# Decode attention with its softmax in two parts and K moved in 8 MB loads

## The chip, the cores and the metric

The kernel runs on 1 core of a Trainium2 chip. The metric is the device time of one execution in microseconds (us). Times of two kernels are compared on the same chip, round by round. PE is the engine for matrix products, DVE is VectorE, ACT is ScalarE, POOL is GpSimd; SyncE issues the loads, and 16 DMA engines move them. PSUM is the memory that PE writes to. PV is the product of the softmax's exponentials with V. A load has landed when the parts of all 16 DMA engines are there.

## The reference, cut to what matters

A decode step of one transformer block, batch 2, one new token, model width 1024, 32 query heads over 4 K/V heads, and a cache of 32768 tokens, all in bf16:

```python
mod = (silu(c) @ w_mod)                       # 12.6 MB of weights
h   = layernorm(x) * (1 + ca) + sa
q   = h @ wq                                  # 8.4 MB
scores = einsum('bhqd,bhkd->bhqk', q, k) * Dh ** -0.5
p   = softmax(scores, axis=-1)
o   = einsum('bhqk,bhkd->bhqd', p, v)         # K and V: 67 MB each
x   = x + ga * (o @ wo)                       # 8.4 MB
...                                           # MLP: w1 and w2, 7.3 MB each
```

The 2 x 4 pairs of batch and K/V head are called groups here, numbered 0 to 7. A group has 8 MB of K and 8 MB of V, and serves 8 query heads. Nothing is read twice, so 178 MB must come from HBM.

## The kernel before

All large loads are issued in one order by SyncE into one arena of 160 KB per partition. K has two buffers of 32 KB, one per half; V has one of 64 KB. A load is issued when the last reader of its place has finished (`frees`):

```python
def add_k(i, hf):   # two loads of 4 MB
    add(("K", i, hf), [2, TPC * D], ...[hf], hf * 32 * KB, f"K{hf}")
def add_v(i):       # one load of 8 MB
    add(("V", i), [NCH, TPC * D], ..., 64 * KB, "V")
for i in range(NBG):
    add_k(i, 0); add_k(i, 1); add_v(i)
# ... wo, w1, w2 follow in the same stream
T.dma("sp", ..., key=cur.sem, writes=[cur.reg], frees=old)
```

In a group, 32 steps transpose 8 blocks of K on PE, copy them out of PSUM (20 on DVE, 12 on ScalarE) and multiply them by q. After each quarter (8 steps) the scores are copied and their maximum is taken. When all four quarters are there, the softmax follows, then PV:

```python
for cc in range(NCH):
    for g8 in range(TPC // 8):
        tr(i, cc, g8)                  # transposes and evacuation
        ...
        qk(*pipe.pop(0))               # three steps later
softmax_1(); softmax_2(); softmax_3()  # one maximum over all 32768 tokens
for cc in range(NCH): exp(cc)
for cc in range(NCH):
    part_sum(cc)
    pv(i, cc)                          # 16 matmuls a quarter
row_sums(); extract(); extract_2(i)
```

## Time and profile before

| | before |
|---|---|
| time, median of 4 runs (range) | 420.06 us (419.99 to 420.11) |
| span of the profiled run | 418.7 us |
| load packets, as a share of 16 DMA engines' span | 98.8% |
| V landings, groups 2 to 7, distance | 38.63 to 38.71 us |
| last weight load landed; end of the kernel | 415.76; 418.69 us |

One row of the page: what the DMA engines moved in each fortieth of the span.

```profile
GB/s 373 450 380 449 448 404 493 398 406 446 441 432 429 423 451 429 419 454 457 391 435 476 407 416 448 438 438 426 438 438 426 416 460 457 377 448 428 424 427 249
```

It stays around 430 (373 to 493) until the last slice. That one holds the 3 us of compute after the last load.

### The profile page before, as it was taken

How to read it: one execution, taken by the hardware profiler on the slowest of the kernel's cores; microseconds unless marked ns; L12 is line 12 of the kernel's file. 1: busy time of each engine (PE TensorE's matmuls, PEld its weight loads, DVE VectorE, ACT ScalarE, POOL GpSimd, SP SyncE). 2: the span in 40 equal slices, each digit the busy share in tenths (PEclk: the TensorE clock that was granted, in tenths of full speed). 3: DMA queues.
4: the chain of work that ended last, by engine and by line, in shares of the span. 5: the costliest groups of instructions: out<-in, count | busy, mean ns of one | idle time of the engine just before them, and what ended most of it. 6: DMA issues, size and time to landing. Idle time of an engine off the chain costs nothing.

```text
span 418.7 us, 11609 instructions
## 1 busy us (share of the span) xinstructions
PE 291.0 (70%) x5183; PEld 231.3 (55%) x5183; DVE 209.6 (50%) x423; ACT 149.4 (36%) x179; POOL 6.8 (2%) x29
## 2 busy tenths in 40 slices
PE   1407449766996895699369957976995699564536
PEld 1104219762993794299149926962894399221214
DVE  1201105546677676467726664766477567620411
ACT  2000015533565364256405632643365166400100
POOL 3000000000000000000000000000000000000000
PEclk9999557986896997799589958986697889576585
DMA  9989999999999999999999999999999999899995
GB/s 373 450 380 449 448 404 493 398 406 446 441 432 429 423 451 429 419 454 457 391 435 476 407 416 448 438 438 426 438 438 426 416 460 457 377 448 428 424 427 249
DMA packets 5581, 178.42 MB, mean 426 GB/s; under 512 B 698, under 2 KB 706, under 8 KB 964
## 3 DMA queue, kind: packets, MB, share of 16 engines
q1 hardware_dynamic: 5572, 178.28, 98.8%
q8 instruction: 8, 0.13, 0.1%
q14 instruction: 1, 0.01, 0.0%
HBM read 178.28 MB, written 0.00 MB: 426 GB/s over the span
## 4 chain that ended last, share of the span: by engine, by line
DMA 71%; PE 24%; DVE 2%; issue 1%; ACT 1%; SPq 1%
DMA V<-in_A_v_cache_dram 39%; DMA wo<-in_A_wo_dram 10%; DMA K<-in_A_k_cache_dram 10%; PE psZ L584 10%; DMA w<-in_B_w_dram 9%; PE psKT L536 8%; DMA wmod<-in_w_mod_dram 4%; PE psS L548 1%; PE psZ L548 1%; PE psS L655 1%; PE psZ L729 1%; PE psZ L469 1%; ACT KT_sb L540 0%; PE psS L469 0%; DVE m1c L553 0%
## 5 line engine op out<-in xcount | busy, mean ns | idle before, releaser
L536 PE MATMUL psKT<-ident,K 128*128 128x128 bf16 x2048 | 163.1, 229 | 11.5 <-DMA K<-in_A_k_cache_dram 11.5
L540 ACT ACTIVATE KT_sb<-psKT 128x1024 bf16<-128x1024 bf16 x96 | 98.2, 1025 | 124.4 <-PE psKT L536 124.4
L542 DVE COPY KT_sb<-psKT 128x1024 bf16<-128x1024 bf16 x160 | 106.7, 688 | 61.6 <-PE psKT L536 61.2
L536 PEld LDWEIGHTS psKT<-ident,K 128*128 128x128 bf16 x2048 | 126.7, 102 | 13.0 <-DMA K<-in_A_k_cache_dram 12.7
L584 PE MATMUL psZ<-V,E_sb 128*32 128x512 bf16 x512 | 46.4, 541 | 23.2 <-DMA V<-in_A_v_cache_dram 20.0
L548 PE MATMUL psS<-qcur,KT_sb 128*128 128x8 bf16 x1024 | 44.7, 167 | 2.2 <-issue 2.2
L584 PEld LDWEIGHTS psZ<-V,E_sb 128*32 128x32 bf16 x512 | 18.7, 130 | 47.7 <-issue 38.8
L548 PE MATMUL psZ<-qcur,KT_sb 128*128 128x8 bf16 x1024 | 43.0, 167 | 2.2 <-issue 1.5
L548 PEld LDWEIGHTS psS<-qcur,KT_sb 128*128 128x128 bf16 x1024 | 40.0, 97 | 2.3 <-issue 2.3
L548 PEld LDWEIGHTS psZ<-qcur,KT_sb 128*128 128x128 bf16 x1024 | 37.9, 96 | 3.4 <-issue 1.6
L572 ACT ACTIVATE E_sb<-S_sb 128x512 bf16<-128x512 f32 x32 | 19.5, 630 | 29.6 <-DVE S_sb L570 29.6
L570 DVE TENSOR_TENSOR S_sb<-S_sb,gmb 128x512 f32<-128x512 f32 x32 | 20.0, 685 | 0.3
L576 DVE TENSOR_REDUCE rs<-E_sb 128x8 f32<-128x512 bf16 x32 | 19.7, 675 | 0.0
L469 PE MATMUL psS<-wmod,inT 128*32 128x512 bf16 x32 | 5.1, 624 | 16.2 <-DMA wmod<-in_w_mod_dram 16.2
L553 DVE TENSOR_REDUCE m1c<-psZ 128x8 f32<-128x512 f32 x16 | 11.1, 693 | 10.2 <-ACT S_sb L552 10.1
L595 DVE RECIPROCAL rinv<-psM 128x1 f32<-128x1 f32 x8 | 1.3, 168 | 27.7 <-PE psM L593 27.7
L605 PE MATMUL psM<-msum,hmat 128*128 128x128 f32 x16 | 4.2, 347 | 13.3 <-DVE msum L600 13.3
L559 PE MATMUL psM<-identf,m 128*8 128x128 f32 x16 | 4.3, 369 | 13.1 <-DVE m L556 13.1
L553 DVE TENSOR_REDUCE m1c<-psS 128x8 f32<-128x512 f32 x16 | 11.1, 693 | 3.2 <-ACT S_sb L552 3.1
L552 ACT ACTIVATE S_sb<-psZ 128x512 f32<-128x512 f32 x16 | 9.5, 595 | 7.5 <-PE psZ L548 7.5
L477 DVE COPY S_sb<-psS 128x512 f32<-128x512 f32 x1 | 0.7, 690 | 22.9 <-PE psS L469 22.9
L469 PEld LDWEIGHTS psS<-wmod,inT 128*32 128x32 bf16 x32 | 1.1, 132 | 19.3 <-DMA wmod<-in_w_mod_dram 18.0
(123 smaller groups left out, 167.5 us busy)
## 6 DMA issues: line engine op xcount, KB each, us to landing
K<-in_A_k_cache_dram SPq DMA_DIRECT2D x16, 4096.0 KB, 27.1
wq<-in_A_wq_dram SPq DMA_DIRECT2D x2, 4096.0 KB, 44.8
wo<-in_A_wo_dram SPq DMA_DIRECT2D x2, 4096.0 KB, 39.0
w<-in_B_w_dram SPq DMA_DIRECT2D x2, 3584.0 KB, 32.5
wmod<-in_w_mod_dram SPq DMA_DIRECT2D x1, 6144.0 KB, 29.8
w<-in_B_w_dram SPq DMA_DIRECT2D x3, 2048.0 KB, 37.8
wmod<-in_w_mod_dram SPq DMA_DIRECT2D x1, 4608.0 KB, 15.8
wmod<-in_w_mod_dram SPq DMA_DIRECT2D x1, 1536.0 KB, 6.0
```

The source lines that it names most:

```text
L469: pe(lambda e, w=it.view, k=k, kk=kk, ch=ch, n=n, q=q: e.matmul(bank[n][32 * q:32 * q + 32, :], lhsT=inT[:, k, :], rhs=w[:, kk, ch * 512:( ...
L536: pe(lambda e, kq=kq, jj=jj, w=kt, t=t: e.transpose(psKT[kq][:, jj * 128:(jj + 1) * 128], w[:, t, :], ident[:, :]), reads=[it.reg, "ident" ...
L540: act(lambda e, src=src: e.activation(KT_sb[g8][:, :, :], src, ACT.Copy), reads=[f"psKT{kq}"], writes=[f"KT_sb{g8}"], sem=f"ev{cc}_{g8}")
L542: dve(lambda e, src=src: e.tensor_copy(KT_sb[g8][:, :, :], src), reads=[f"psKT{kq}"], writes=[f"KT_sb{g8}"], sem=f"ev{cc}_{g8}")
L548: pe(lambda e, t=t, jj=jj: e.matmul(ps[:, t * HPG:(t + 1) * HPG], lhsT=KT_sb[g8][:, jj, :], rhs=qcur[:, :], start=True, stop=True), reads= ...
L552: act(lambda e: e.activation(Sc, ps.rearrange("p (t h) -> p h t", h=HPG), ACT.Copy), reads=[preg], writes=[f"S_sb_{cc}"], sem=f"sc{cc}")
L553: dve(lambda e: e.tensor_reduce(m1c[:, :, cc], ps.rearrange("p (t h) -> p h t", h=HPG), AX.X, ALU.max), reads=[preg], writes=[f"m1c{cc}"])
L559: pe(lambda e: e.matmul(psM[0:HPG, 0:128], lhsT=m1[:, :], rhs=identf[:, :], start=True, stop=True), reads=["m1", "identf"], writes=["psM"])
L570: dve(lambda e: e.tensor_tensor(Sc, Sc, gmb[:, :].unsqueeze(2).to_broadcast([128, HPG, TPC]), ALU.subtract), reads=[f"S_sb_{cc}", "gmb"], ...
L572: act(lambda e: e.activation(Ec, Sc.rearrange("p h (u t) -> p u h t", t=4), ACT.Exp, scale=SCALE), reads=[f"S_sb_{cc}"], writes=[f"E_sb_{c ...
L576: dve(lambda e: e.tensor_reduce(rs4[:, :, cc], Ec.rearrange("p u h t -> p h u t"), AX.XY, ALU.add), reads=[f"E_sb_{cc}"], writes=[f"rs4_{c ...
L584: pe(lambda e, t4=t4, tg=tg, q=q: e.matmul(psO[32 * q:32 * q + 32, :], lhsT=E_sb[:, tg // 4, :, :].rearrange("p h t -> p (h t)"), rhs=vt[: ...
```

## The change

Its intent is to move K in 8 MB loads, like V, and to make up for what that costs in time for the compute. A whole K in one buffer has to be free as a whole: so DVE copies the second half aside (four copies of 4096 elements per partition), and the transposes of the last two quarters read the copy. Compute then starts only when all 8 MB are there. So that V's buffer is free in time all the same, the first three quarters get their own maximum, and their PV runs beside the softmax of the last quarter. Both PV sums are joined with weights exp(m_part - m).

```diff
-    def add_k(i, hf):
-        add(("K", i, hf), [2, TPC * D], ...[hf], hf * 32 * KB, f"K{hf}")
+KEEP = {(0, 1): 0, (0, 5): 1, (1, 3): 2, (2, 1): 3}      # step after which each copy stands
+    def add_k(i):
+        if i:
+            add(("K", i), [NCH, TPC * D], rows, 0, "K", view=kv)      # 8 MB
+        else:                                                         # group 0: two halves
+            add(("K", i), ... rows[:, 0:2, :], 0, sem="K", ...)
+            add(("K2", i), ... rows[:, 2:4, :], 32 * KB, sem="K2", ...)
...
+    def keep(i, n):
+        dve(lambda e: e.tensor_copy(kc[:, n // 2, lo:lo + 32 * D], kv[:, 2 + n // 2, lo:lo + 32 * D]), ...)
...
-            act(... S_sb copy of the quarter ...)
-            dve(... maximum of the quarter ...)
+            dve(... maximum of the quarter ...)
+            act(... S_sb copy of the quarter ...)
...
-        softmax_1(); softmax_2(); softmax_3()
-        for cc in range(NCH): exp(cc)
-        for cc in range(NCH):
-            part_sum(cc); pv(i, cc)
-        row_sums(); extract(); extract_2(i)
+        exp(0); exp(1)                  # the maximum of quarters 0 to 2 was taken during quarter 3
+        ...                             # rest of the scores
+        exp(2); pv(i, 0); max_2(1); pv(i, 1); max_3(1); exp(3); weights(); pv(i, 2)
+        ...                             # part sums, weights_2
+        row_sums(); extract(0); pv(i, 3); row_sums_2(); extract(1); extract_2(i)
```

Evacuations are now 16 on DVE and 16 on ScalarE per group, and some weight loads at the end have other places in the arena.

More of the change, by code (lines that the diff above doesn't have):

```diff
@@ L34 @@
 RING = 160 * 1024
+KC_AT = 128 * 1024
 AHEAD = ("sc2", "sc3", "pk", "ac")
 WMOD_ITEMS = ((0, 1), (1, 4), (4, 8))
-W2_ITEMS = ((0, 8, 96), (8, 16, 112), (16, 24, 128), (24, 27, 144), (27, 28, 150))
-EVAC_PATTERN = ("dve", "act", "dve", "act", "dve", "dve", "act", "dve")
+W2_ITEMS = ((0, 8, 96), (8, 16, 112), (16, 24, 0), (24, 27, 16), (27, 28, 22))
+KEEP = {(0, 1): 0, (0, 5): 1, (1, 3): 2, (2, 1): 3}
 class Tracker:
@@ L211, in wait @@
             def wait(w):
+                if w[1] == 0:
+                    return eng.wait_ge(self.sem[w[0]], w[2])
                 eng.wait_ge(self.sem[w[0]], val[w[1:]] if w[1:] in val else it * w[1] + w[2])
@@ L250, in bass_adaLN_cond__gqa_block_cached__mixer_channel_mlp__decode_kernel @@
     T = Tracker(nc)
-    T.step["pe"], T.step["dve"] = 72, 14
+    T.step["pe"], T.step["dve"] = 74, 18
     def sb(name, shape, dtype=FP32):
@@ L305, in bass_adaLN_cond__gqa_block_cached__mixer_channel_mlp__decode_kernel @@
     diag = sb("diag", [HPG, HPG])
-    gmb = sb("gmb", [128, HPG])
+    gmb = sb("gmb", [128, 2, HPG])
+    mx = sb("mx", [128, HPG])
+    dw = sb("dw", [128, 2, HPG])
+    wt = sb("wt", [128, 2, HPG])
+    wh = sb("wh", [128, 2, HPG])
+    wp = sb("wp", [128, 2])
+    mkw = sb("mkw", [128, 2, 4])
     rowsum = sb("rowsum", [128, HPG])
-    rs4 = sb("rs4", [128, HPG, NCH])
+    rs4 = sb("rs4", [128, HPG, NCH - 1])
+    rs2 = sb("rs2", [128, 2, HPG])
     rinv = sb("rinv", [128, 1])
@@ L333, in bass_adaLN_cond__gqa_block_cached__mixer_channel_mlp__decode_kernel, with add @@
     KB = 1024
-    def add(key, shape, src, off, slot=None):
+    def add(key, shape, src, off, slot=None, sem=None, view=None):
         it = Item()
@@ L340, in add @@
         it.reg = f"it{it.n}"
-        it.sem = f"d_{slot or it.reg}"
-        it.view = views.get(slot)
+        it.sem = f"d_{sem or slot or it.reg}"
+        it.view = views.get(slot) if view is None else view
         if it.view is None:
@@ L349, in add @@
         by_key[key] = it
-    def add_k(i, hf):
-        add(("K", i, hf), [2, TPC * D], A_k_cache[i % 2, i // 2].rearrange("(p h c t) d -> h p c (t d)", h=2, c=2, p=128)[hf], hf * 32 * KB, f"K{hf}")
+    kv = nc.alloc_sbuf_tensor_at("kv", [128, NCH, TPC * D], BF16, offset=abase)
+    def add_k(i):
+        rows = A_k_cache[i % 2, i // 2].rearrange("(p c t) d -> p c (t d)", c=NCH, p=128)
+        if i:
+            add(("K", i), [NCH, TPC * D], rows, 0, "K", view=kv)
+            by_key["K2", i] = by_key["K", i]
+        else:
+            add(("K", i), [2, TPC * D], rows[:, 0:2, :], 0, sem="K", view=kv[:, 0:2, :])
+            add(("K2", i), [2, TPC * D], rows[:, 2:4, :], 32 * KB, sem="K2", view=kv[:, 2:4, :])
+            T.key("d_K2")
+            T.step["d_K2"] = 0
     def add_v(i):
@@ L364, in bass_adaLN_cond__gqa_block_cached__mixer_channel_mlp__decode_kernel @@
     for i in range(NBG):
-        add_k(i, 0)
-        add_k(i, 1)
+        add_k(i)
         add_v(i)
-    for m, off in enumerate((128, 0)):
+    for m, off in enumerate((0, 32)):
         add(("wo", m), [16, DM], A_wo[m * 2048:(m + 1) * 2048, :].rearrange("(p j) n -> p j n", j=16), off * KB)
     w1_v = B_w1.rearrange("(p k) n -> p k n", k=KT8)
-    for m, off in enumerate((32, 64)):
+    for m, off in enumerate((128, 64)):
         add(("w1", m), [4, F], w1_v[:, 4 * m:4 * m + 4, :], off * KB)
@@ L376, in bass_adaLN_cond__gqa_block_cached__mixer_channel_mlp__decode_kernel @@
     w2_of = {j: (m, j - j0) for m, (j0, j1, off) in enumerate(W2_ITEMS) for j in range(j0, j1)}
+    kc = nc.alloc_sbuf_tensor_at("kc", [128, 2, TPC * D], BF16, offset=abase + KC_AT)
     pos = [0]
@@ L384, in need @@
             old = [o.reg for o in stream[:cur.n] if o.off < cur.off + cur.nbytes and cur.off < o.off + o.nbytes]
+            if cur.n > by_key["V", NBG - 1].n and cur.off < KC_AT + 32 * KB and KC_AT < cur.off + cur.nbytes:
+                old += [f"kc{n}" for n in range(4)]
             if len(cur.view.shape) == 3:
@@ L516, in bass_adaLN_cond__gqa_block_cached__mixer_channel_mlp__decode_kernel @@
                reads=[f"qrow{n}", "ident"] + EREG, writes=["psM"], mark=(i == 3))
-    dve(lambda e: e.tensor_copy(qT[:, :, :], psM[:, 0:64].rearrange("p (b h) -> p b h", b=2)), reads=["psM"], writes=["qT"], sem="mo")
+    dve(lambda e: e.tensor_copy(qT[:, :, :], psM[:, 0:64].rearrange("p (b h) -> p b h", b=2)), reads=["psM"], writes=["qT"], sem="mo1")
     for name in AHEAD:
@@ L521, in bass_adaLN_cond__gqa_block_cached__mixer_channel_mlp__decode_kernel @@
         T.raw("pe", lambda e, name=name: e.sem_inc(T.sem[name], T.step.get(name, 1)))
+    T.wait("dve", writes=[it.reg for it in stream if it.key[0] in ("wmod", "wq")])
     T.wait("pe", reads=["ident", "identf", "onesf", "hmat"], writes=["psS0", "psS1", "psO", "psM"] + [f"psKT{q}" for q in range(NPKT)])
@@ L530, in tr @@
     def tr(i, cc, g8):
-        it = need("K", i, cc // 2)
-        kt = it.view[:, cc % 2, :].rearrange("p (t d) -> p t d", d=D)
+        it = need("K", i)
+        kt = (kv[:, cc, :] if cc < 2 else kc[:, cc - 2, :]).rearrange("p (t d) -> p t d", d=D)
+        k_reg = it.reg if cc < 2 else f"kc{2 * (cc - 2) + g8 // 4}"
         kq = g8 % NPKT
@@ L536, in tr @@
             pe(lambda e, kq=kq, jj=jj, w=kt, t=t: e.transpose(psKT[kq][:, jj * 128:(jj + 1) * 128], w[:, t, :], ident[:, :]),
-               reads=[it.reg, "ident"], writes=[f"psKT{kq}"], mark=(jj == 7))
+               reads=[k_reg, "ident"], writes=[f"psKT{kq}"], mark=(jj == 7))
         src = psKT[kq][:, :].rearrange("p (a n) -> p a n", a=8)
-        if EVAC_PATTERN[g8] == "act":
+        if g8 % 2:
             act(lambda e, src=src: e.activation(KT_sb[g8][:, :, :], src, ACT.Copy), reads=[f"psKT{kq}"], writes=[f"KT_sb{g8}"], sem=f"ev{cc}_{g8}")
@@ L542, in tr @@
             dve(lambda e, src=src: e.tensor_copy(KT_sb[g8][:, :, :], src), reads=[f"psKT{kq}"], writes=[f"KT_sb{g8}"], sem=f"ev{cc}_{g8}")
+    def keep(i, n):
+        it = need("K2", i)
+        lo = n % 2 * 32 * D
+        dve(lambda e: e.tensor_copy(kc[:, n // 2, lo:lo + 32 * D], kv[:, 2 + n // 2, lo:lo + 32 * D]), reads=[it.reg], writes=[f"kc{n}"], sem=f"kc{n}")
     def qk(i, cc, g8):
@@ L551, in qk @@
             Sc = S_sb[:, :, cc * TPC:(cc + 1) * TPC]
+            dve(lambda e: e.tensor_reduce(m1c[:, :, cc], ps.rearrange("p (t h) -> p h t", h=HPG), AX.X, ALU.max), reads=[preg], writes=[f"m1c{cc}"], sem=f"mc{cc}")
             act(lambda e: e.activation(Sc, ps.rearrange("p (t h) -> p h t", h=HPG), ACT.Copy), reads=[preg], writes=[f"S_sb_{cc}"], sem=f"sc{cc}")
-            dve(lambda e: e.tensor_reduce(m1c[:, :, cc], ps.rearrange("p (t h) -> p h t", h=HPG), AX.X, ALU.max), reads=[preg], writes=[f"m1c{cc}"])
@@ L555, in softmax_1 @@
-    def softmax_1():
-        dve(lambda e: e.tensor_reduce(m1[:, :], m1c[:, :, :], AX.X, ALU.max), reads=[f"m1c{cc}" for cc in range(NCH)], writes=["m1"], sem="m1")
-    def softmax_2():
-        pe(lambda e: e.matmul(psM[0:HPG, 0:128], lhsT=m1[:, :], rhs=identf[:, :], start=True, stop=True), reads=["m1", "identf"], writes=["psM"])
-        dve(lambda e: e.tensor_reduce(gm[:, :], psM[0:HPG, 0:128], AX.X, ALU.max), reads=["psM"], writes=["gm"], sem="gm")
-        dve(lambda e: e.tensor_scalar(diag[:, :], identf[0:HPG, 0:HPG], gm[:, 0:1], None, ALU.mult), reads=["identf", "gm"], writes=["diag"], sem="dg")
@@ L563, in softmax_3, with max_1, max_2 @@
-    def softmax_3():
+    def max_1():
+        dve(lambda e: e.tensor_reduce(m1[:, :], m1c[:, :, 0:NCH - 1], AX.X, ALU.max), reads=[f"m1c{cc}" for cc in range(NCH - 1)], writes=["m1"], sem="m1")
+    def max_2(part):
+        src, reg = (m1[:, :], "m1") if part == 0 else (m1c[:, :, NCH - 1], f"m1c{NCH - 1}")
+        pe(lambda e: e.matmul(psM[0:HPG, 0:128], lhsT=src, rhs=identf[:, :], start=True, stop=True), reads=[reg, "identf"], writes=["psM"])
+        dve(lambda e: e.tensor_reduce(gm[:, :], psM[0:HPG, 0:128], AX.X, ALU.max), reads=["psM"], writes=["gm"], sem=f"gm{part}")
+        dve(lambda e: e.tensor_scalar(diag[:, :], identf[0:HPG, 0:HPG], gm[:, 0:1], None, ALU.mult), reads=["identf", "gm"], writes=["diag"], sem=f"dg{part}")
@@ L564, in softmax_3, with max_3 @@
+    def max_3(part):
         pe(lambda e: e.matmul(psM[:, 128:128 + HPG], lhsT=onesf[0:HPG, :], rhs=diag[:, :], start=True, stop=True), reads=["onesf", "diag"], writes=["psM"])
-        dve(lambda e: e.tensor_copy(gmb[:, :], psM[:, 128:128 + HPG]), reads=["psM"], writes=["gmb"])
+        dve(lambda e: e.tensor_copy(gmb[:, part, :], psM[:, 128:128 + HPG]), reads=["psM"], writes=[f"gmb{part}"], sem=f"gb{part}")
     def exp(cc):
+        part = cc // (NCH - 1)
         Sc = S_sb[:, :, cc * TPC:(cc + 1) * TPC]
@@ L569, in exp @@
         Ec = E_sb[:, cc * TPC // 4:(cc + 1) * TPC // 4, :, :]
-        dve(lambda e: e.tensor_tensor(Sc, Sc, gmb[:, :].unsqueeze(2).to_broadcast([128, HPG, TPC]), ALU.subtract),
-            reads=[f"S_sb_{cc}", "gmb"], writes=[f"S_sb_{cc}"], sem=f"sb{cc}")
+        dve(lambda e: e.tensor_tensor(Sc, Sc, gmb[:, part, :].unsqueeze(2).to_broadcast([128, HPG, TPC]), ALU.subtract),
+            reads=[f"S_sb_{cc}", f"gmb{part}"], writes=[f"S_sb_{cc}"], sem=f"sb{cc}")
         act(lambda e: e.activation(Ec, Sc.rearrange("p h (u t) -> p u h t", t=4), ACT.Exp, scale=SCALE), reads=[f"S_sb_{cc}"], writes=[f"E_sb_{cc}"], sem=f"ex{cc}")
@@ L575, in part_sum, with weights, weights_2 @@
         Ec = E_sb[:, cc * TPC // 4:(cc + 1) * TPC // 4, :, :]
-        dve(lambda e: e.tensor_reduce(rs4[:, :, cc], Ec.rearrange("p u h t -> p h u t"), AX.XY, ALU.add), reads=[f"E_sb_{cc}"], writes=[f"rs4_{cc}"])
+        dst, reg = (rs4[:, :, cc], f"rs4_{cc}") if cc < NCH - 1 else (rs2[:, 1, :], "rs2_1")
+        dve(lambda e: e.tensor_reduce(dst, Ec.rearrange("p u h t -> p h u t"), AX.XY, ALU.add), reads=[f"E_sb_{cc}"], writes=[reg])
+    def weights():
+        dve(lambda e: e.tensor_tensor(mx[:, :], gmb[:, 0, :], gmb[:, 1, :], ALU.max), reads=["gmb0", "gmb1"], writes=["mx"])
+        dve(lambda e: e.tensor_tensor(dw[:, :, :], gmb[:, :, :], mx[:, :].unsqueeze(1).to_broadcast([128, 2, HPG]), ALU.subtract), reads=["gmb0", "gmb1", "mx"], writes=["dw"], sem="dw")
+        act(lambda e: e.activation(wt[:, :, :], dw[:, :, :], ACT.Exp, scale=SCALE), reads=["dw"], writes=["wt"], sem="wt")
+    def weights_2():
+        dve(lambda e: e.tensor_tensor(wh[:, :, :], wt[:, :, :], hsel[:, :].unsqueeze(1).to_broadcast([128, 2, HPG]), ALU.mult), reads=["wt", "hsel"], writes=["wh"])
+        dve(lambda e: e.tensor_reduce(wp[:, :], wh[:, :, :], AX.X, ALU.add), reads=["wh"], writes=["wp"])
+        dve(lambda e: e.tensor_tensor(mkw[:, :, :], mk4[:, :].unsqueeze(1).to_broadcast([128, 2, 4]), wp[:, :].unsqueeze(2).to_broadcast([128, 2, 4]), ALU.mult),
+            reads=["mk4", "wp"], writes=["mkw"])
     def pv(i, cc):
@@ L580, in pv @@
         vt = it.view[:, cc, :]
+        last = cc == NCH - 1
+        acc, reg = (psS[0], "psS0") if last else (psO, "psO")
         for t4 in range(TPC // 4):
@@ L583, in pv, with row_sums_2 @@
             q = t4 % 4
-            pe(lambda e, t4=t4, tg=tg, q=q: e.matmul(psO[32 * q:32 * q + 32, :], lhsT=E_sb[:, tg // 4, :, :].rearrange("p h t -> p (h t)"),
+            pe(lambda e, t4=t4, tg=tg, q=q: e.matmul(acc[32 * q:32 * q + 32, :], lhsT=E_sb[:, tg // 4, :, :].rearrange("p h t -> p (h t)"),
                                                     rhs=vt[:, t4 * 512:(t4 + 1) * 512],
-                                                    start=(cc == 0 and t4 < 4), stop=(cc == NCH - 1 and t4 >= TPC // 4 - 4),
+                                                    start=((last or cc == 0) and t4 < 4), stop=(cc >= NCH - 2 and t4 >= TPC // 4 - 4),
                                                     skip_group_check=True),
-               reads=[it.reg, f"E_sb_{cc}"], writes=["psO"], mark=(t4 == TPC // 4 - 1))
+               reads=[it.reg, f"E_sb_{cc}"], writes=[reg], mark=(t4 == TPC // 4 - 1))
     def row_sums():
-        dve(lambda e: e.tensor_reduce(rowsum[:, :], rs4[:, :, :], AX.X, ALU.add), reads=[f"rs4_{cc}" for cc in range(NCH)], writes=["rowsum"])
+        dve(lambda e: e.tensor_reduce(rs2[:, 0, :], rs4[:, :, :], AX.X, ALU.add), reads=[f"rs4_{cc}" for cc in range(NCH - 1)], writes=["rs2_0"])
+        dve(lambda e: e.tensor_tensor(wh[:, :, :], rs2[:, :, :], wt[:, :, :], ALU.mult), reads=["rs2_0", "rs2_1", "wt"], writes=["wh"])
+        dve(lambda e: e.tensor_tensor(rowsum[:, :], wh[:, 0, :], wh[:, 1, :], ALU.add), reads=["wh"], writes=["rowsum"])
         dve(lambda e: e.tensor_copy(rsum16[:, :, :, :], rowsum[:, :].unsqueeze(1).unsqueeze(3).to_broadcast([128, 2, HPG, 8])), reads=["rowsum"], writes=["rsum16"], sem="rs")
+    def row_sums_2():
         pe(lambda e: e.matmul(psM[:, 144:145], lhsT=rsum16.rearrange("p g h e -> p (g h e)"), rhs=onesf[:, 0:1], start=True, stop=True),
@@ L595, in row_sums, with extract @@
         dve(lambda e: e.reciprocal(rinv[:, :], psM[:, 144:145]), reads=["psM"], writes=["rinv"], sem="rv")
-    def extract():
-        dve(lambda e: e.tensor_scalar(msum[:, :], psO[:, 0:128], mk4[:, 0:1], None, ALU.mult), reads=["psO", "mk4"], writes=["msum"])
-        for q in range(1, 4):
-            dve(lambda e, q=q: e.scalar_tensor_tensor(out=msum[:, :], in0=psO[:, q * 128:(q + 1) * 128], scalar=mk4[:, q:q + 1], in1=msum[:, :],
-                                                      op0=ALU.mult, op1=ALU.add), reads=["psO", "mk4", "msum"], writes=["msum"], sem="mo" if q == 3 else None)
+    def extract(part):
+        acc, reg = ((psO, "psO"), (psS[0], "psS0"))[part]
+        for q in range(4):
+            if part == 0 and q == 0:
+                dve(lambda e: e.tensor_scalar(msum[:, :], acc[:, 0:128], mkw[:, 0, 0:1], None, ALU.mult), reads=[reg, "mkw"], writes=["msum"])
+            else:
+                dve(lambda e, q=q: e.scalar_tensor_tensor(out=msum[:, :], in0=acc[:, q * 128:(q + 1) * 128], scalar=mkw[:, part, q:q + 1], in1=msum[:, :],
+                                                          op0=ALU.mult, op1=ALU.add), reads=[reg, "mkw", "msum"], writes=["msum"], sem=f"mo{part}" if q == 3 else None)
     def extract_2(i):
@@ L624, in bass_adaLN_cond__gqa_block_cached__mixer_channel_mlp__decode_kernel @@
                 tr(i, cc, g8)
+                if (cc, g8) in KEEP:
+                    keep(i, KEEP[cc, g8])
                 pipe.append((i, cc, g8))
@@ L629, in bass_adaLN_cond__gqa_block_cached__mixer_channel_mlp__decode_kernel @@
                     qk(*pipe.pop(0))
+                if (cc, g8) == (3, 2):
+                    max_1()
+                if (cc, g8) == (3, 4):
+                    max_2(0)
+                if (cc, g8) == (3, 6):
+                    max_3(0)
+        exp(0)
+        exp(1)
         while pipe:
             qk(*pipe.pop(0))
-        softmax_1()
-        softmax_2()
-        softmax_3()
-        for cc in range(NCH):
-            exp(cc)
+        exp(2)
+        pv(i, 0)
+        max_2(1)
+        pv(i, 1)
+        max_3(1)
+        exp(3)
+        weights()
+        pv(i, 2)
         for cc in range(NCH):
             part_sum(cc)
-            pv(i, cc)
+            if cc == 0:
+                weights_2()
         row_sums()
-        extract()
+        extract(0)
+        pv(i, 3)
+        row_sums_2()
+        extract(1)
         extract_2(i)
```

## The prediction

> **What bounds the kernel now.** I read the page first, for the engines and the DMA row, then the chain of waits, then the timeline of the queue that issues the loads, then the trace's records of single DMA packets and of landings.
>
> The page, its DMA row (busy share of the 16 DMA engines in 40 slices), its packet count, its queue row and the chain's shares:
>
> ```profile
> PE 291.0 (70%) x5183; PEld 231.3 (55%) x5183; DVE 209.6 (50%) x423; ACT 149.4 (36%) x179; POOL 6.8 (2%) x29
> ...
> DMA  9989999999999999999999999999999999899995
> ...
> DMA packets 5581, 178.42 MB, mean 426 GB/s; under 512 B 698, under 2 KB 706, under 8 KB 964
> ...
> q1 hardware_dynamic: 5572, 178.28, 98.8%
> ...
> DMA 71%; PE 24%; DVE 2%; issue 1%; ACT 1%; SPq 1%
> ```
>
> The reader is to see that no compute engine is near its limit, while the load queue's packets fill 98.8% of 16 engines over the whole span: 0.988 x 418.7 = 413.5 us of DMA work. The last slice holds nearly all that is missing. Counting how many packets are in flight, I find 16 from 1.9 us until 414 us: about 1.9 us are empty at the start, 3.6 us in the last 20, and at most 0.14 us in any 20 us between. The compute that follows the last landing (415.8 to 418.7 us) ends the kernel.
>
> The chain of waits says 24% PE, which could mislead. In order of time, one group of it reads:
>
> ```profile
> 252.82 32.15 DMA V<-in_A_v_cache_dram
> 284.97 0.14 issue
> 285.11 5.79 PE psZ L584 x64
> 290.94 32.74 DMA V<-in_A_v_cache_dram
> ```
>
> It seems that PV (5.8 us) lies on the path, because the V buffer is single and its next load is issued when PV has read it. But 8 MB need 8 packets of 64 KB per DMA engine at 2.418 us each = 19.3 us, and this load is shown as 32.7 us from issue to landing. The other 13.4 us it stands in the queue behind K loads that were issued before it:
>
> ```profile
> 252.82 0.33 SPq L389 DMA_DIRECT2D V<-in_A_v_cache_dram  x1
> 267.10 10.68 SPq L389 DMA_DIRECT2D K<-in_A_k_cache_dram  x2
> 290.94 0.33 SPq L389 DMA_DIRECT2D V<-in_A_v_cache_dram  x1
> ```
>
> (Start, time from the first issue to the end of the last, what.) The two K issues at 267.1 and about 277.4 come while V is still moving (it lands at 284.97), and V's next issue at 290.94 comes while those two move (they land at 294.65 and 304.38). So the queue never runs dry. PV, softmax and scores have 13 us of room in every group. The kernel is bound by DMA bytes, and its floor is these 413.5 us.
>
> **What the Trainium skill says.** (1) "DMA: Bandwidth & Descriptors", section "Where 436 GB/s comes from", gives 16 ports x 32 B x 850 MHz = 435.2 GB/s as the ceiling. The trace agrees: a 64 KB packet takes 2418 ns, 16 x 65536 B / 2418 ns = 433.6 GB/s; a 32 KB packet takes 1213 ns, 432.2 GB/s. (2) The same page, section "Anatomy of one DMA", gives about 2.0 us of fixed cost per DMA, mostly the receipt at the end. In this trace the cost does not appear in the rate, because another load is always queued: from the first K half's landing to the second's are 9.68 us, and 8 packets x 1.213 = 9.70. (3) "VectorE: DVE Perf Modes", section "The perf-mode tier table", puts a dense bf16 SBUF to SBUF copy at 4 elements a cycle (693 ns for 2048). The kernel before has no such copy; its only bf16 SBUF copy has a strided source and took 1054 ns for 1024. So this stands unconfirmed. (4) "TensorE: Matmul & The Clock Gate", Part 1, says that PE falls to half clock after some 3.4 us idle and needs about as long to recover. The chain agrees: in the first group eight transposes took 0.87 us at first and 0.47 later.
>
> **The change part by part.** Call the landing of group i's whole K time 0. In the steady state V of that group lands at 19.3 and the next K at 38.6: the landings of V are 38.63 to 38.71 us apart in the trace.
>
> *K in one load, seven times (group 0 keeps two).* Per load and DMA engine, 16 packets of 32 KB become 8 of 64 KB: 16 x 1213 - 8 x 2418 = 64 ns saved; one completion packet less (9 ns). 7 x 73 ns = 0.5 us. A second reckoning from landings: both K halves together take 9.668 + 9.684 = 19.35 us, V 19.33, means over the last six groups; 0.027 x 7 = 0.2 us. I take 0.35 us. This is all that lies on the path that sets the end. Bytes, order of loads, and the compute after the last weight load stay as they were; the weight loads only change places in memory.
>
> *When K's buffer is free again.* Half of K is transposed in place, the other half is copied aside by four DVE copies of 4096 bf16; the last copy stands after the 18th of 32 transpose groups. The next K must be issued about 1 us ahead of V's landing (the first load of all was issued at 0.74 and its first packet moved at 1.75), so by 18.3. In the trace the first 16 transpose groups need 9.8 to 12.0 us from the landing on (178.6 to 188.4; 294.65 to 306.67; the slower ones start at half clock). 18/16 of that is 11 to 13.5; plus one copy, estimated from the skill's figure as 4096/4/0.96 GHz + 0.16 = 1.2 us: issue at 12 to 15. Margin 3 to 6 us. DVE work up to there: 9 evacuations x 0.688 + 0.69 + 4 x 1.2 = 11.7 us, beside PE's 11 to 13.5, so DVE nearly keeps up with PE and may cost a microsecond of the margin.
>
> *When V's buffer is free.* Compute now begins when all of K is there, 9.7 us later than before; that eats most of the 13.4 us. The split softmax gives some back. Scores end at 9.8 to 12.0 plus 10.7 (the K timeline's row) = 20.5 to 22.7. Then, for the last quarter alone: maximum 0.69, one subtraction ahead of it 0.69, two PE round trips about 0.6 each, 0.29 + 0.22 + 0.17 for the small DVE steps, subtraction 0.69, exp 0.63, 16 PV matmuls 5.79/4 = 1.45: about 6.0. PV of the first three quarters (4.3 us) runs beside this. V free at 26.5 to 29, needed by 37.6: margin 9 us. Without the split it would be 5.1 us from the last score to PV (127.66 to 132.72 in the chain) and 5.8 of PV, so 31.5 to 34: it would fit as well.
>
> *Group 0.* Its first copy needs K's second half, which lands at 72.3 (the first at 62.4), and DVE waits there with the evacuations behind it. From 72.3 on DVE has about 11 us of work up to the fourth copy, and PE 12 to 13 transpose groups at 0.65 to 1.06 us with one 1.5 us stall that the chain shows as "issue". K of group 1 is then issued at 84 to 88; V of group 0 lands at 91.7, so it is needed by 90.7. Margin 3 to 6 us.
>
> *Added small work*: about 12 DVE instructions of 0.17 to 0.35 us (the weights) and one activation per group. All of it lies inside the time that PE and DVE wait for V or K anyway. The evacuations go from 20 DVE and 12 ACT to 16 and 16 per group; ACT then has 4 x 1.025 + 0.6 = 4.7 us per quarter against PE's 8 x 0.65 = 5.2, so PE stays the pace of the scores.
>
> Sum: 420.06 - 0.35 + 0 = 419.7 us.
>
> **The rivals.** (a) Each load costs a fixed 2 us, and seven fewer save 14 us: 406 us. For it: the skill's fixed cost. Against it: the landing distances, which leave no room for it, and 16 packets in flight at every moment. (b) The split shortens the chain of scores, softmax and PV; if that chain set the period, 5 us x 8 groups = 40 us would go, 380 us. For it: the chain of waits, where PV and softmax appear. Against it: the 13.4 us in the queue, and 413.5 us of packets that stay. (c) The copies run at one element per cycle, 4096/0.96 = 4.3 us each. Then DVE needs about 24 us up to the fourth copy against 18.3 allowed, and each group opens a hole of 6 us: 420 + 7 x 6 = 462 us. Against it: the skill's table; operands are dense and bf16. (d) Only group 0 is late: one hole of 1 to 3 us, 421 to 423 us. For it: the smallest margin of all, with instruction fetches in the first pass of the loops. (e) A transfer hidden anyway: my main case.
>
> **Range and chances.** The main case gives 419.5 to 419.9. Runs of one kernel lie 0.12 us apart here, other runs may differ by a few tenths more; (d) gets one chance in eight and pulls the upper side. Eight in ten: 419.0 to 420.8. Over 2% faster would need 411.7 us, below the packet time, so 0.01. Over 2% slower needs 428.5 us, case (c) or a hole in most groups: 0.03. Within 2%: 0.96.
>
> **What the changed profile would show.** Right: the DMA row still 9s, mean near 427 GB/s, q1's share 98 to 99%; some 900 packets fewer (7 x 128); V landings 38.6 us apart; K issued 12 to 16 us after K's landing, V 26 to 29; four copies of about 1.2 us a group; PE, DVE idle for several us ahead of each K landing. Wrong: a slice of the DMA row at 8 or less between 60 and 400 us, V or K issued after the landing of the load ahead, copies above 2 us, or a distance of landings above 39 us. A group that starts at half clock throughout would cut the margins, not the time. If K packets of 64 KB took longer than V's 2418 ns, the 0.35 us would be gone.

## The result, and the profile after

The changed kernel takes 422.09 us (median of 4 runs, 421.81 to 423.76), the kernel before 420.06. The ratio is 1.0056, 95% interval 1.003 to 1.0083. (A ratio is the mean time of one kernel's runs over that of the other's of the same rounds, so not quite the ratio of the medians.) That is within 2%, as forecast, but 2.0 us slower where 0.35 us less was forecast, and outside the range of 419.0 to 420.8. Note also the spread: 0.12 us before, 1.95 us now. The profile is of the fastest of the four runs; it can explain its 1.8 us, and the run of 423.76 us has no trace.

The page of the changed kernel (run of 421.81 us, span 420.5), with the lines that answer to those of before:

```profile
PE 288.7 (69%) x5215; PEld 232.8 (55%) x5215; DVE 244.3 (58%) x535; ACT 181.8 (43%) x219; POOL 6.8 (2%) x29
...
DMA  9989999999999999999999999999999999999994
GB/s 375 449 387 435 449 418 472 413 457 415 430 443 405 443 405 449 443 411 449 436 418 461 424 436 449 411 443 449 405 430 461 405 430 461 400 421 440 420 427 197
DMA packets 4573, 178.42 MB, mean 424 GB/s; under 512 B 586, under 2 KB 594, under 8 KB 852
...
q1 hardware_dynamic: 4564, 178.28, 98.3%
...
DMA 57%; PE 30%; DVE 6%; ACT 3%; issue 3%; SPq 0%; ACTq 0%; DVEq 0%
```

The DMA row is full until the last slice, much as before, and the packets are the same work as before: added up over the trace and divided by 16 they take 413.5 us in both kernels. The clear difference in these rows is at the very end: the last slice moved at 197 GB/s instead of 249. A mean over 16 engines hides what happened; one has to look at the engines singly. The trace records when each of the 16 engines finishes its part of a load (the load's semaphore rises by one each time). The first, the median (midway between the 8th and the 9th) and the last of these 16 times, for five loads:

| load | before: first, median, last | after: first, median, last |
|---|---|---|
| V of group 1 | 128.54, 128.96, 130.31 | 128.57, 129.33, 130.21 |
| K of group 2 (all) | 147.92, 148.31, 149.66 | 148.50, 149.12, 150.21 |
| V of group 7 | 360.63, 361.06, 362.37 | 361.10, 361.92, 362.75 |
| w1, first half | 388.56, 389.23, 390.16 | 388.98, 389.78, 392.11 |
| last piece of w2 | 414.11, 415.24, 415.76 | 414.54, 415.32, 417.53 |

Read the last row first. The median engine ends at 415.2 and 415.3 us. The last engine is 0.52 us behind it before, and 2.21 us after; the kernel ends 2.93 us after the last one before, and 2.95 us after. So the loss of this run, 417.53 - 415.76 = 1.77 us, is that of the latest DMA engines. They are two: one ends at 417.53 and one at 417.10; the other 14 are through by 415.48, before the last engine of the kernel before. (The mean of the 16 rose from 414.97 to 415.42.) The latest engine's loss came in two bites: K of group 2 (20.00 us from the landing of V, where before took 19.35), and w1 (10.03 us from the load ahead to this one, 8.48 before).

Where do single engines lose time? The packet records name no engine, but an engine's packet starts where its last one ended, so each engine can be followed through the trace. Two kinds of gap appear. *Instruction fetches*: 16 KB of program code moves on queue 8, takes 0.94 us of one engine and lengthens the data packet beside it by about 0.49. That engine is 1.4 us late from then on, and in no trace here do the others take over its share of a load (the last experiment shows this best). Before had eight of these after 20 us, as far as the packets can be followed each on another engine; after had eight too. The first half of w1 met one in both kernels (started at 386.1 and 387.1). *Starts of loads*: in the changed kernel, one engine had a gap of 2.0 us and a packet 0.3 us too long at 130.3 us, another a packet 1.5 us too long at 128.5, and others lost 0.1 to 0.5 us. In the kernel before, apart from fetches, no engine lost more than 0.15 us at the start of a K or V load. The engine with 2.3 us lost then met the instruction fetch of 387.1 us, which makes 3.7 us in all. The one with the long packet at 128.5 us met the fetch of 409.8 us, which makes about 3: these are the two that end last.

What stands at 128 to 130 us is the start of group 2's K load. The timeline of the load queue (start, time, what):

```profile
105.91 0.33 SPq L411 DMA_DIRECT2D V<-in_A_v_cache_dram  x1
126.62 0.33 SPq L411 DMA_DIRECT2D kv<-in_A_k_cache_dram  x1
143.12 0.33 SPq L411 DMA_DIRECT2D V<-in_A_v_cache_dram  x1
164.81 0.33 SPq L411 DMA_DIRECT2D kv<-in_A_k_cache_dram  x1
```

K was issued at 126.62, and the first engine was through with V at 128.57, 1.95 us later. I call this distance the *lead* of a load. In the kernel before the same loads read:

```profile
102.47 0.33 SPq L389 DMA_DIRECT2D V<-in_A_v_cache_dram  x1
116.18 10.68 SPq L389 DMA_DIRECT2D K<-in_A_k_cache_dram  x2
137.97 0.33 SPq L389 DMA_DIRECT2D V<-in_A_v_cache_dram  x1
```

Its first half of K for group 2 was issued at 116.18, 12.36 us before the first engine was through with V (128.54), and no K or V load had a lead under 6.7 us. In the changed kernel the K loads of groups 1 to 7 have 4.05, 1.95, 3.00, 3.41, 2.57, 2.98 and 3.45 us, and V of group 1 has 3.29. (The first load of wo, whose place has changed, has 2.51 us, but took no longer than before: 9.72 us on the mean engine in both kernels.)

Why so late? The chain of waits of the changed kernel, in order of time:

```profile
111.04 0.79 PE psM L657 x2
111.83 3.41 PE psKT L560 x32
...
117.22 0.47 PE psKT L560 x8
...
126.62 23.59 DMA kv<-in_A_k_cache_dram
```

K of group 1 landed at 110.92. PE was still at the end of group 0 until 111.83, and then started at half clock (32 transposes in 3.41 us; later eight take 0.47, so 32 would take 1.9; the granted clock was 0.50 from 111.8 to 115.3 us and 1.00 from 119.0 to 126.6). The fourth copy ended, and K was issued, 15.7 us after the landing. From group 2 on it was 14.2 to 15.1. The copies themselves are as fast as estimated from the Trainium skill ("VectorE: DVE Perf Modes", section "The perf-mode tier table"), 1.218 us against 1.2:

```profile
L571 DVE COPY kc<-kv 128x4096 bf16<-128x4096 bf16 x32 | 39.0, 1218 | 7.9 <-DMA kv<-in_A_k_cache_dram 7.9
```

### The profile page after: what moved, and what is told of

Read it like the earlier page. It is cut to its first block, busy times and chain, and to the rows that moved or that the text cites. A ratio compares the mean times of both kernels' runs of the same rounds, so it can differ in the third digit from the quotient of the medians.

```text
span 420.5 us, 11898 instructions
## 1 busy us (share of the span) xinstructions
PE 288.7 (69%) x5215; PEld 232.8 (55%) x5215; DVE 244.3 (58%) x535; ACT 181.8 (43%) x219; POOL 6.8 (2%) x29
## 4 chain that ended last, share of the span: by engine, by line
DMA 57%; PE 30%; DVE 6%; ACT 3%; issue 3%; SPq 0%; ACTq 0%; DVEq 0%
DMA kv<-in_A_k_cache_dram 43%; PE psKT L560 19%; DMA w<-in_B_w_dram 7%; DMA wmod<-in_w_mod_dram 7%; PE psS L577 3%; ACT KT_sb L564 3%; PE psZ L577 2%; DVE m1c L581 2%; PE psZ L629 1%; DVE msum L652 1%; DVE rs L608 1%; PE psS L724 1%; PE psZ L491 1%; PE psZ L798 1%; PE psS L491 0%
## 5 line engine op out<-in xcount | busy, mean ns | idle before, releaser
L564 ACT ACTIVATE KT_sb<-psKT 128x1024 bf16<-128x1024 bf16 x128 | 128.3, 1024 | 99.0 <-PE psKT L560 99.0
L566 DVE COPY KT_sb<-psKT 128x1024 bf16<-128x1024 bf16 x128 | 87.3, 688 | 63.4 <-PE psKT L560 63.3
L560 PE MATMUL psKT<-ident,kv 128*128 128x128 bf16 x1024 | 89.6, 246 | 14.4 <-DMA kv<-in_A_k_cache_dram 14.4
L560 PEld LDWEIGHTS psKT<-ident,kv 128*128 128x128 bf16 x1024 | 72.7, 112 | 16.3 <-DMA kv<-in_A_k_cache_dram 16.3
L560 PE MATMUL psKT<-ident,kc 128*128 128x128 bf16 x1024 | 77.9, 218 | 0.0
L560 PEld LDWEIGHTS psKT<-ident,kc 128*128 128x128 bf16 x1024 | 58.1, 97 | 1.9 <-issue 1.7
L571 DVE COPY kc<-kv 128x4096 bf16<-128x4096 bf16 x32 | 39.0, 1218 | 7.9 <-DMA kv<-in_A_k_cache_dram 7.9
L629 PE MATMUL psZ<-V,E_sb 128*32 128x512 bf16 x384 | 26.9, 398 | 2.0 <-ACT E_sb L603 2.0
L582 ACT ACTIVATE S_sb<-psS 128x512 f32<-128x512 f32 x16 | 9.6, 597 | 16.6 <-DVE m1c L581 16.6
L629 PEld LDWEIGHTS psZ<-V,E_sb 128*32 128x32 bf16 x384 | 10.6, 99 | 8.7 <-ACT E_sb L603 2.7
## 6 DMA issues: line engine op xcount, KB each, us to landing
wmod<-in_w_mod_dram SPq DMA_DIRECT2D x1, 4608.0 KB, 15.7
```

Of the source, the lines that this page charges most:

```text
L560: pe(lambda e, kq=kq, jj=jj, w=kt, t=t: e.transpose(psKT[kq][:, jj * 128:(jj + 1) * 128], w[:, t, :], ident[:, :]), reads=[k_reg, "ident"] ...
L564: act(lambda e, src=src: e.activation(KT_sb[g8][:, :, :], src, ACT.Copy), reads=[f"psKT{kq}"], writes=[f"KT_sb{g8}"], sem=f"ev{cc}_{g8}")
L566: dve(lambda e, src=src: e.tensor_copy(KT_sb[g8][:, :, :], src), reads=[f"psKT{kq}"], writes=[f"KT_sb{g8}"], sem=f"ev{cc}_{g8}")
L571: dve(lambda e: e.tensor_copy(kc[:, n // 2, lo:lo + 32 * D], kv[:, 2 + n // 2, lo:lo + 32 * D]), reads=[it.reg], writes=[f"kc{n}"], sem=f" ...
L582: act(lambda e: e.activation(Sc, ps.rearrange("p (t h) -> p h t", h=HPG), ACT.Copy), reads=[preg], writes=[f"S_sb_{cc}"], sem=f"sc{cc}")
L629: pe(lambda e, t4=t4, tg=tg, q=q: e.matmul(acc[32 * q:32 * q + 32, :], lhsT=E_sb[:, tg // 4, :, :].rearrange("p h t -> p (h t)"), rhs=vt[: ...
```

## The experiments

The theory to test is 1: a load that is issued too shortly before the engines run out of work makes some of them stall, and the kernel ends with the latest of them. Its rivals are 2: 8 MB loads in 64 KB packets are slower; and 3: the DVE copies disturb the DMA's writes into SBUF. For each run the table gives the first, median and last engine at the last piece of w2, and the end of the profiled execution.

| run | time, median (range) us | ratio to before, 95% | profiled run us | last w2: first, median, last | end |
|---|---|---|---|---|---|
| before | 420.06 (419.99-420.11) | | 420.02 | 414.11, 415.24, 415.76 | 418.69 |
| after | 422.09 (421.81-423.76) | 1.0056 (1.0030-1.0083) | 421.81 | 414.54, 415.32, 417.53 | 420.48 |
| a_early | 419.91 (419.59-421.50) | 1.0002 (0.9989-1.0014) | 421.47 | 414.25, 415.29, 417.19 | 420.15 |
| b_late | 425.26 (423.16-427.13) | 1.0121 (1.0098-1.0143) | 425.73 | 418.51, 419.28, 421.45 | 424.40 |
| c_two | 423.46 (422.03-424.92) | 1.0077 (1.0060-1.0094) | 424.92 | 417.59, 418.56, 420.58 | 423.55 |
| d_split | 419.92 (419.87-420.03) | 0.9998 (0.9985-1.0011) | 419.87 | 413.95, 415.29, 415.59 | 418.54 |
| f_order | 419.99 (419.71-420.19) | 0.9999 (0.9986-1.0012) | 419.99 | 413.83, 414.89, 415.69 | 418.67 |
| h_order | 421.10 (420.07-423.68) | 1.0043 (1.0017-1.0068) | 420.71 | 414.43, 415.25, 416.44 | 419.39 |
| b_mid | 420.71 (420.43-423.69) | 1.0015 (1.0002-1.0028) | 423.69 | 416.89, 417.62, 419.43 | 422.36 |
| g_fetch | 431.82 (431.75-431.93) | 1.0281 (1.0268-1.0295) | 431.75 | 414.17, 415.20, 427.49 | 430.41 |

The kernel before was at 420.01 to 420.02 (medians) beside the experiments, so runs of different rounds can be set side by side. All runs gave correct results. In each line, end minus last engine is 2.9 to 3.0 us.

**a_early: the copies earlier.**

```diff
-KEEP = {(0, 1): 0, (0, 5): 1, (1, 3): 2, (2, 1): 3}
+KEEP = {(0, 0): 0, (0, 4): 1, (1, 0): 2, (1, 4): 3}
```

> The changed kernel with only the four copies of K's second half placed earlier (after transpose groups 1, 5, 9 and 13 instead of 2, 6, 12 and 18 of 32), so that the next K load is issued as soon as the first half is transposed. Theory 1 (late issue: in the changed kernel the next K load is issued only 1.6 to 3.2 us before the fastest DMA engines run out of V packets, some engines then stand idle, and one of them ends up last at the end): K is issued 2 to 3 us earlier, no long packets and no gaps at the starts of K loads, time 419.6 to 420.3. Theory 2 (64 KB packets or 8 MB K loads are themselves slower): stays at 421.8 to 423.8. Theory 3 (DVE copies disturb the DMA writes): stays at 421.8 to 423.8.

Four of six runs took 419.59 to 419.94 us, two 421.5. The leads of K loads rose to 3.5 to 6.3 us, and no K load cost the mean engine over 0.2 us any more. The 64 KB packets, the 8 MB loads and the copies are all still there, so theories 2 and 3 fall as causes of the loss. The two runs of 421.5 us are outside what I expected. The profiled run was one of them, and shows what I had not foreseen: V of group 1, issued at 106.79 with a lead of 2.31 us, opened a gap of 2.1 us in one engine at 110.9, and that engine met the fetch of 385.7 us.

**b_late: the kernel before, with late K loads and nothing else.**

```diff
-T.dma("sp", ..., key=cur.sem, writes=[cur.reg], frees=old)
+T.dma("sp", ..., key=cur.sem, writes=[cur.reg], frees=old,
+      after=["gm"] if cur.key[0] == "K" and cur.key[1] >= 3 and cur.key[2] == 0 else [])
```

> The kernel before with one wait added: from the fourth group on, the first K half's load waits until the softmax maximum of the group before is known (it ends 2.9, 3.3, 1.7, 1.9 and 1.2 us before the fastest DMA engines run out of V packets in the five cases). No copies, 32 KB packets, 4 MB loads, one softmax. Theory 1: gaps and long packets at the starts of the last three of these loads, time 420.5 to 423. Theories 2 and 3: 420.0 to 420.2, as before.

It took 425.26 us, 5.2 more than the kernel before, with 4 MB loads in 32 KB packets and without copies. Theory 1 alone forecast a loss, and the loss was larger than forecast. The timeline of the load queue has the five late loads (the two K issues are now 0.4 us apart):

```profile
164.98 0.80 SPq L389 DMA_DIRECT2D K<-in_A_k_cache_dram  x2
...
204.01 0.80 SPq L389 DMA_DIRECT2D K<-in_A_k_cache_dram  x2
...
244.42 0.80 SPq L389 DMA_DIRECT2D K<-in_A_k_cache_dram  x2
...
284.82 0.81 SPq L389 DMA_DIRECT2D K<-in_A_k_cache_dram  x2
...
323.72 0.80 SPq L389 DMA_DIRECT2D K<-in_A_k_cache_dram  x2
```

Their leads were 2.31, 2.03, 0.95, 1.04 and 1.90 us. The mean engine lost 0.06, 0.80, 1.63, 0.98 and 0.95 us at them. Here even the median engine ends 4 us later.

**c_two: the changed kernel, each K in two loads of 4 MB issued together.**

```diff
-        if i:
-            add(("K", i), [NCH, TPC * D], rows, 0, "K", view=kv)
+        add(("K", i), [2, TPC * D], rows[:, 0:2, :], 0, sem="K", view=kv[:, 0:2, :])
+        add(("K2", i), [2, TPC * D], rows[:, 2:4, :], 32 * KB, sem="K2", view=kv[:, 2:4, :])
...
+            if cur.key[0] == "K" and cur.key[1]:
+                old.append(by_key["K2", cur.key[1] - 1].reg)     # same moment of issue
```

> The changed kernel with each 8 MB K load cut into two 4 MB loads (32 KB packets) that are issued one right after the other at the moment at which the one was issued; the transposes wait for both. Theory 1: still late, still slow, 421.3 to 424. Theory 2: back to 420.0 to 420.5. Theory 3: slow as well.

Slow again, 423.46 us: smaller loads and packets do not help, which is against theory 2. It is no clean pair with the changed kernel, though. Its group 0 also waits for both halves, so its first loads are later still (leads of 2.47, 1.21 and 1.11 us), and these three loads alone cost its mean engine 2.4 us. So it is the slower of the two.

**d_split: the split softmax alone**, with K in two halves as before and no copies.

```diff
...                                     # the K loads as in c_two, for each half its own moment of issue
-        kt = (kv[:, cc, :] if cc < 2 else kc[:, cc - 2, :]).rearrange("p (t d) -> p t d", d=D)
+        kt = kv[:, cc, :].rearrange("p (t d) -> p t d", d=D)
...
-                if (cc, g8) in KEEP:
-                    keep(i, KEEP[cc, g8])
```

> The softmax in two parts alone: K in two halves as before, each with its own buffer and issued when its half is transposed, no copies. Theory 1: every load is issued well ahead (over 6 us), time 419.9 to 420.4. If the split softmax itself (more instructions, more instruction fetches over the DMA engines) costs the time: 421 to 424.

419.92 us, with a spread of 0.16. Within the interval of the ratio (0.15%) the split costs nothing and gains nothing; neither do the new places of the weight loads. No lead was under 6 us.

**h_order and f_order: ScalarE's copy ahead of DVE's maximum**, alone and with later-placed copies that do not stop DVE in group 0.

```diff
-            dve(... maximum of the quarter ...)
             act(... S_sb copy of the quarter ...)
+            dve(... maximum of the quarter ...)
-KEEP = {(0, 1): 0, (0, 5): 1, (1, 3): 2, (2, 1): 3}      # f_order only
+KEEP = {(0, 6): 0, (1, 0): 1, (1, 2): 2, (1, 5): 3}
...                                     # and one name more in AHEAD, in both runs
```

> The changed kernel with ScalarE's copy ahead of DVE's maximum alone, copies where they were. Theory 1: K is issued about 1.5 us earlier than in the changed kernel (margin about 3 to 4.5 us), V several us earlier; gaps rare or short: 419.5 to 421. If the order of the two does not matter for the time: 421.8 to 423.8.

> The changed kernel with two moves, both to issue loads earlier: the four copies stand after transpose groups 7, 9, 11 and 14 (so that in group 0 DVE no longer waits for K's second half with the evacuations behind it), and ScalarE copies the scores of a quarter before DVE takes their maximum, as in the kernel before (so that the evacuations behind the copy don't wait for DVE). Theory 1 (late issue): every load is issued 4 us or more before the fastest DMA engines run dry, no gaps, 419.3 to 419.9 and little spread from run to run, under the kernel before. If 8 MB K loads have another cost: 420.0 or more, or a spread over 0.5 us.

The order alone moved the K of group 2 ahead by 0.5 us, counted from the landing of K ahead, and the later ones not at all, where I had reckoned with 1.5; the leads of K were 2.45 to 4.4 us, and the time 421.10 us with a spread of 3.6: between the kernel before and the changed one, as the leads say. With the copies moved as well, all leads were 3.2 us or more, no load lost time, and the spread fell to 0.5 us. But the leads are not the 4 us that I expected, and 419.99 us is the kernel before, not less than it. The gain of the larger loads is there, but small. From V to V (groups 2 to 7) the mean engine takes 38.65 us, against 38.68 in before and in d_split, which have the smaller loads; that is 0.2 us for seven groups, and the mean engine ends at 414.78 us, 0.19 us ahead of before's 414.97. (The medians, 414.89 and 415.24, say less: in both kernels the 8th and 9th engine, between which they lie, are about half a microsecond apart.) The last engine ends at 415.69 against 415.76, so little of it reaches the time.

**b_mid: as b_late, but held about 1 us less.**

```diff
-      after=["gm"] if cur.key[0] == "K" and ...
+      after=["m1"] if cur.key[0] == "K" and ...
```

> The kernel before with the first K half's load, from the fourth group on, held until the softmax maximum's first step (about 1 us earlier than in the run that held it until the maximum was known; margins of about 3.8, 4.2, 2.6, 2.9 and 1.9 us). Theory 1: smaller and fewer gaps than there, none at the first two of the five loads, 420.3 to 422.5, between the kernel before and 425.3. A theory without a dependence on the margin: 420.0 or 425.3.

420.71 us, between before and b_late; one run of six at 423.69, and that is the profiled one, whose leads were 2.77, 1.87, 1.89, 1.71 and 2.21 us, shorter than I expected. Taking the nine traces of before, after, a to d, f, h and b_mid together, each load of K or V with a lead under 6 us gives a point (lost: the mean over engines of the time from the load ahead to this one, less 19.33 us, or 9.66 for half a K):

| lead, us | loads | lost by the mean engine, us: mean (least to most) |
|---|---|---|
| under 1.5 | 4 | 1.04 (0.63 to 1.63) |
| 1.5 to 2.4 | 11 | 0.62 (0.06 to 1.11) |
| 2.4 to 3.1 | 10 | 0.20 (0.03 to 0.81) |
| 3.1 to 6 | 46 | 0.00 (-0.03 to 0.20) |

The largest two in the last row (0.17 and 0.20) are the K loads of group 1, which fall among the instruction fetches of the first pass. So about 3.1 us of lead are needed here.

**g_fetch: does one engine's delay really set the end?** The kernel before with 330 one-element memsets per group on idle GpSimd. They add instructions to fetch, and keep GpSimd busy for 94.6 us instead of 6.8.

```diff
...
                     next_q(i)
+                    for k in range(330):
+                        T.inst("pool", lambda e, k=k: e.memset(pad[:, 330 * i + k:330 * i + k + 1], 0.0), ...)
```

> The kernel before with 330 one-element memsets per group on idle GpSimd: only more instructions to fetch. In the traces each fetch of 16 KB of instructions delays one of the 16 DMA engines by 1.4 us for good, each time another engine, and the last landing follows the engine that lost most. Theory: 8 to 12 more fetches; as long as no engine is hit twice the end stays at 420.0 to 420.3; if the round wraps and an engine is hit twice, 421.2 to 421.8 and that engine ends 1.4 us after the others. If fetches don't matter: 420.0 to 420.2 and no such engine.

My expectation of its size was wrong, and the result is the clearest of all: 431.82 us. The page:

```profile
PE 294.3 (68%) x5183; PEld 234.5 (54%) x5183; DVE 209.8 (49%) x423; ACT 149.4 (35%) x179; POOL 94.6 (22%) x2669
...
DMA  9999999999999999999999999999999999999950
GB/s 366 438 414 437 438 435 469 392 419 422 455 420 435 461 434 417 429 458 416 405 466 427 415 438 464 434 405 426 442 412 438 466 428 410 433 421 425 430 237 19
...
q8 instruction: 8, 0.13, 0.1%
q14 instruction: 22, 0.18, 0.1%
```

GpSimd's code came in 22 fetches of 8 KB on queue 14 (one before), 0.1% of the DMA time, and it did not go round: all of them delayed the same engine, by about 0.6 us each (0.30 of their own and some 0.3 on the packet beside them). The median engine ended at 415.20 us, as before; the last one at 427.49, 11.7 us later than before's last, and the kernel 11.7 us later. From 416 to 427 us one engine worked alone: that is the 19 GB/s of the last slice. It is not GpSimd's own work that held the kernel up, for the other 15 engines were through by 416.02 us.

## Why the prediction was wrong

*The bound* (DMA bytes, 413.5 us of packets, compute hidden): right. Packets were 413.5 us again (the product 0.988 x 418.7 gives 413.7; the packets added up give 413.5), and d_split showed that softmax and PV are off the path. The room in the kernel before was smaller than "13 us ... in every group": measured as a lead, V of group 1 had 6.74 us. And the section "Anatomy of one DMA", on which rival (a) rests, is written for loads issued from GpSimd; the loads here are issued from SyncE.

*The saving of the 8 MB loads*, 0.35 us: somewhat high. f_order showed 0.2 us on the mean engine, which is the second of the two reckonings; the first, from packet times (0.5 us), was not reached. The step from there to the time was wrong too: it took the engines as one. The time follows the last engine, and f_order's last engine gained 0.07 us.

*"The next K must be issued about 1 us ahead of V's landing ... so by 18.3"*: this is the step that failed, and twice in one term. The lead needed is about 3.1 us, not 1.0: I had measured the latency of the first load, on idle engines, and took it for that of a load behind a full queue. And the clock runs from the first engine that is through, not from the landing, which is the last: 128.57 against 130.21 us in V of group 1. Put together, K has to be issued by about 19.3 - 1.6 - 3.1 = 14.6 us after K's landing, not by 18.3.

*"Issue at 12 to 15"*: 15.7 for group 1, 14.2 to 15.1 later. The upper end was right for most: as PE now waits before each group, every group starts at half clock (granted clock 0.50), and the fourth copy stands behind an evacuation on DVE. The estimate of 1.2 us per copy held. With the two terms the margin was not 3 to 6 us but -1 to +0.4.

*"When V's buffer is free"*: forecast 26.5 to 29 us after K's landing, measured 30.7 to 32.2. That is 1.7 to 3.2 us over the top of the range, but without effect: the leads of V were 5.4 to 6.3 us from group 2 on.

*Group 0*: K of group 1 forecast at 84 to 88, issued at 85.74. Right, and harmless.

*The rivals*: (a), (b) and (c) did not happen. (d), one hole of 1 to 3 us and 421 to 423 us, had the right size and the wrong place: the hole opened at the K load that group 1 releases, not group 0. I gave it one chance in eight, because I reckoned the margin with 1 us. *"V landings above 39 us apart"* was named as the sign of being wrong, and it came: 130.21 to 169.52, 39.3 us.

*What stays open*: that the same engine is hit by a late start and by a later fetch was followed in the traces of after and a_early. That this is more than chance (engines without a fetch so far run dry first, and the late fetches fell on engines without one) is argued, not shown. Nor does a run show which engine a late issue will delay, and so how much a single execution loses. The mechanism of the stall between issue and first packet under load was not tested.

## What to carry to other kernels

When DMA is the bound and its busy row is full, look at the 16 engines singly: here every load landed with its slowest engine, and a delay of one engine stayed to the end. Issue a load so early that even the fastest engine still has some 3 us of older work, and count this from the first engine's end, not from the landing. With loads always queued, the larger load was worth 0.03 us each here, and that isn't worth a buffer that comes free later.

## What the Trainium skill lacked or had wrong

- "DMA: Bandwidth & Descriptors", section "Anatomy of one DMA", gives one fixed cost of about 2.0 us per DMA, for loads issued from GpSimd; for loads issued from SyncE, as here, the page has a first-byte latency of about 0.6 us. Neither says how far ahead a load must be queued behind others. These runs: none of 46 loads with a lead over 3.1 us lost more than 0.20 us, and 15 loads with leads under 2.4 us lost 0.06 to 1.63 us on the mean engine, single engines over 2 us.
- The same page, section "Queues, rings and completion order", says that an engine takes turns between its queues packet by packet. The traces agree (a gap of 0.9 us between two data packets at a fetch of 16 KB), but the page does not say what instruction fetches cost a data stream, and "Runtime: NRT & Kernel Launch", section "Instruction fetch mechanics", calls the cost of a 16 KB block "mostly hidden" with no word on other loads. Here it was 1.4 us of one engine for 16 KB, about 0.6 us for 8 KB, and the 22 of GpSimd's queue all on one engine (+11.7 us on the kernel).
- "DMA: Bandwidth & Descriptors" says in passing, under an explanation that it calls unconfirmed, that a bulk load runs at the pace of its slowest engine. No page was found that says that a delay of one engine adds up over many loads, or that the busy row hides it: in g_fetch 415.20 us for the median engine, 427.49 for the last, and nines in the row up to its last two slices.
